# Two of five blocks of K transposed by permutes and DMA instead of TensorE, with a zero column and a warm-up on constants

## The chip, the core and the metric

The kernel runs on one core of a Trainium2 chip. The metric is device time in microseconds (us), the median of several runs. The engines are named as in the profile: PE (TensorE matmul) and PEld (its weight loads), DVE (VectorE), ACT (ScalarE), POOL (GpSimd) and SP (SyncE, which here only issues DMAs).

## What is computed

The input is one sequence of 2048 positions with 640 channels. A long convolution over the sequence is followed by a dense layer with Mish:

```
x  = A_q
h  = x + layernorm(x) * y                  # y, per channel:
     k_shift = sum over t of 4 taps: k shifted by t * shift_k[:, t]
     kv      = k_shift * v
     y       = causal_conv(kv, ssm_k) + kv * ssm_D     # length 2048, by FFT in the reference
h2 = h + mish(layernorm(h) @ w1 + b1) @ w2 # F = 1728
```

## The kernel before

Position s is 16 p + a, with p the partition (128) and a = 0 to 15. Channels are split into five blocks of 128 (`NDC`), and these into three chunks: blocks 0 and 1, blocks 2 and 3, block 4. The convolution is a two-stage transform written as matmuls:

- `k1pe`/`k1ev`: the filter `ssm_k` (loads d_n0 to d_n4) is transposed by PE into PSUM and copied out ("evicted") by DVE or ACT. `s1kpe`/`s1kev` is its first transform stage, `s2kpe`/`s2kev` its second, which multiplies by the table G (loads d_g0 to d_g7).
- `ktpe`/`ktev`: K, the raw k, lies with positions on partitions (loads d_k0 to d_k3). For the shift along the sequence PE transposes it, eight 128x128 tiles to a unit, x for the first half of a (h = 0) and y for the second (h = 1). Each block b gets a buffer `kt_s[b]` with three parts of 128 columns for each of eight tiles: the two halves, and the second half moved on by one column with a zero in front, which POOL copies (`ktsh`).
- `wsh`: the four taps as small banded matrices, a product of a mask and the coefficients (`coef`), ten of them on POOL. `kspe` multiplies `kt_s` by them in PE, and `kv` multiplies the result by v on DVE, from PSUM into the buffer that held the raw k. So kv also waits until the raw k has been read.
- `s1vpe`, `s2vpe`: the two stages for kv. `sw`: DMAs that exchange odd and even partitions of the transformed filter (`sw0` for chunk 0 in four pieces, `sw1` and `sw2` in two). `p1`, `p2`: the products of the two spectra, on POOL and DVE. `i1pe`, `i2p`: the inverse stages.
- Then, by groups of positions, the layernorms, `m1pe` (w1), `hb` (Mish on ACT), `m2pe` (w2), `res` and the store. Fourteen DMA transposes (`trd`) bring the normalised rows into the layout that m1pe needs; they are there before and after.

Every operation is an `OP` with a name, engines that may run it, and what it depends on. The text `ORDER` gives each name and an engine (t PE, v DVE, a ACT, p POOL, d the DMA queue on SP, s that on ACT). `_schedule` walks through it and gives each a start by the file's own figures, and the instructions are issued in the order of these starts. Each engine and each queue runs its own in that order. A pair of names ending in x and y is one `unit` in two PSUM banks; there are eight banks (`R_PS`), so PE can be at most eight evictions ahead.

`wm` is a burst of eleven matmuls on a zeroed tile (`wz`, a DVE memset) ahead of everything else on PE. `dcpe` then needs d_dr, and `k1pe0y` needs d_n0.

## Time and profile before

| | us |
|---|---|
| median of 3 runs | 221.82 |
| lowest and highest | 221.41, 222.13 |
| span of the profiled execution | 219.6 |
| PE busy in it | 212.6 |
| DVE busy | 145.1 |
| ACT busy | 133.1 |
| POOL busy | 75.6 |

The span is the time from the first to the last instruction of one execution; no other time is listed for that execution, and the median of the runs stands 2.2 us above its span. Matmuls are pipelined, so that PE counts as busy while one streams in and another drains, and it can also be called busy when it runs at less than its best rate. The table by stretch shows in which part of the kernel which engine has no idle time. The chain of work that ended last is followed back from the last instruction, at each step to what released it. The loads fill the DMA engines up to about 35 us.

### The profile page before, as it was taken

How to read it: one execution, taken by the hardware profiler on the slowest of the kernel's cores; microseconds unless marked ns; L12 is line 12 of the kernel's file. 1: busy time of each engine (PE TensorE's matmuls, PEld its weight loads, DVE VectorE, ACT ScalarE, POOL GpSimd, SP SyncE). 2: the span in 40 equal slices, each digit the busy share in tenths (PEclk: the TensorE clock that was granted, in tenths of full speed). 3: DMA queues.
4: the chain of work that ended last, by engine and by line, in shares of the span. 5: the costliest groups of instructions: out<-in, count | busy, mean ns of one | idle time of the engine just before them, and what ended most of it. 6: DMA issues, size and time to landing. Idle time of an engine off the chain costs nothing.

```text
span 219.6 us, 6285 instructions
## 1 busy us (share of the span) xinstructions
PE 212.6 (97%) x2611; PEld 157.8 (72%) x2618; DVE 145.1 (66%) x324; ACT 133.1 (61%) x265; POOL 75.6 (34%) x112
## 2 busy tenths in 40 slices
PE   8999999999989999999999999999999999999993
PEld 2899889999879999899876644566554444656672
DVE  0799999999999999989699889883210000213023
ACT  2488899999999999997881178600036475300000
POOL 0079997089844007124883371411000000000000
PEclk9999999999999999999999999999999999999999
DMA  6999993417999906996004401552720000000113
GB/s 213 375 419 414 412 403 130 98 23 174 192 263 285 380 10 217 325 359 105 0 0 64 91 14 45 50 103 60 86 79 19 0 3 0 0 0 3 54 60 125
DMA packets 32876, 31.03 MB, mean 141 GB/s; under 512 B 19024, under 2 KB 29264, under 8 KB 32464
## 3 DMA queue, kind: packets, MB, share of 16 engines
q1 hardware_dynamic: 32384, 30.43, 46.3%
q8 instruction: 20, 0.33, 0.7%
q10 hardware_dynamic: 368, 0.20, 0.4%
q14 instruction: 8, 0.07, 0.1%
q0 software_dynamic: 96, 0.00, 0.0%
HBM read 20.47 MB, written 2.62 MB: 105 GB/s over the span
## 4 chain that ended last, share of the span: by engine, by line
PE 76%; ACT 11%; DVE 5%; issue 3%; SPq 2%; DMA 1%; DVEq 0%; ACTq 0%
PE ps L943 26%; PE ps L910 26%; ACT uk L428 8%; PE ps L813 4%; ACT uv L428 3%; PE ps L756 3%; PE ps L757 3%; PE ps L635 2%; PE ps L561 2%; PE ps L473 2%; PE ps L590 2%; DMA xa<-uk 1%; DVE ra L613 1%; PE ps L931 1%; DVE uv L716 1%
## 5 line engine op out<-in xcount | busy, mean ns | idle before, releaser
L910 PE MATMUL ps<-G 128*128 128x512 bf16 (+1 forms) x319 | 58.5, 336 | 0.3
L943 PE MATMUL ps<-rn,uv 128*128 128x320 bf16 (+2 forms) x415 | 58.5, 299 | 0.1
L915 ACT ACTIVATE uv<-ps,b1s 128x512 bf16<-128x512 f32 (+1 forms) x65 | 35.6, 607 | 36.6 <-PE ps L910 34.8
L943 PEld LDWEIGHTS <-uv 128*128 128x128 bf16 x416 | 39.2, 98 | 18.5 <-issue 1.6
L910 PEld LDWEIGHTS <-G 128*128 128x128 bf16 x325 | 31.1, 98 | 24.0 <-issue 0.9
L428 ACT CAST uk<-ps 128x512 bf16<-128x512 f32 (+1 forms) x91 | 47.2, 703 | 1.9 <-PE ps L562 1.4
L948 DVE TENSOR_TENSOR xb<-ps,xb 128x320 bf16<-128x320 f32 (+2 forms) x12 | 5.6, 488 | 42.6 <-ACT uv L915 24.3
L428 ACT CAST uv<-ps 128x512 bf16<-128x512 f32 (+2 forms) x54 | 28.6, 766 | 0.0
L430 DVE CAST uk<-ps 128x512 bf16<-128x512 f32 (+2 forms) x32 | 20.1, 661 | 0.6 <-ACT uk L428 0.5
L756 PE MATMUL ps<-a,uv 128*128 128x128 bf16 x160 | 18.7, 219 | 0.4 <-DVE uv L716 0.3
L756 PEld LDWEIGHTS <-uv 128*128 128x128 bf16 x160 | 17.8, 114 | 0.9 <-DVE uv L716 0.5
L837 POOL TENSOR_TENSOR r<-ve,mhalf 128x1 f32<-128x1 f32 x16 | 9.7, 613 | 25.0 <-DVE ve L834 24.9
L430 DVE CAST uv<-ps 128x512 bf16<-128x512 f32 (+2 forms) x28 | 17.2, 669 | 0.2 <-ACT uv L428 0.2
L948 DVE TENSOR_TENSOR xa<-ps,xa 128x320 bf16<-128x320 f32 x12 | 5.6, 486 | 14.0 <-PE ps L943 13.9
L613 DVE TENSOR_TENSOR ra<-ps,rb 128x512 bf16<-128x512 f32 x20 | 12.9, 683 | 0.3 <-ACT uv L428 0.3
L720 POOL TENSOR_TENSOR rn<-rn,uv 128x1024 bf16<-128x1024 bf16 x5 | 10.6, 2127 | 7.2 <-PE ps L697 7.2
L697 PE MATMUL ps<-uv,G 128*128 128x64 bf16 (+1 forms) x256 | 12.2, 197 | 0.8 <-ACT uv L428 0.6
L662 PE MATMUL ps<-uk,G 128*128 128x160 bf16 x128 | 12.4, 230 | 0.3 <-ACT uk L428 0.2
L697 PEld LDWEIGHTS <-G 128*128 128x128 bf16 x256 | 10.8, 96 | 1.4 <-issue 1.0
L428 ACT CAST rb<-ps 128x512 bf16<-128x512 f32 (+1 forms) x30 | 11.3, 464 | 0.7 <-PE ps L813 0.4
L561 PE MATMUL ps<-cst,ra 128*64 128x128 bf16 x160 | 10.7, 219 | 0.4
L562 PE MATMUL ps<-cst,ra 128*64 128x128 bf16 x160 | 10.9, 222 | 0.0
(111 smaller groups left out, 375.7 us busy)
## 6 DMA issues: line engine op xcount, KB each, us to landing
G<-tab_g SPq DMA_DIRECT2D x8, 512.0 KB, 14.1
rn<-in_A_ssm_k_dram SPq DMA_DIRECT2D x5, 512.0 KB, 6.3
ra<-in_A_k_dram SPq DMA_DIRECT2D x4, 640.0 KB, 11.4
rb<-in_A_v_dram SPq DMA_DIRECT2D x2, 1280.0 KB, 13.9
G<-in_B_w_dram SPq DMA_DIRECT2D x5, 432.0 KB, 7.3
rn<-in_B_w_dram SPq DMA_DIRECT2D x1, 2080.0 KB, 13.4
rn<-uk SPq DMA_DIRECT2D x8, 256.0 KB, 4.3
rb<-uk SPq DMA_DIRECT2D x8, 256.0 KB, 4.5
```

Source lines behind the costliest of these rows:

```text
L428: nc.scalar.copy(o, i)
L430: nc.vector.tensor_copy(o, i)
L561: nc.tensor.matmul(ps[0:64, k, :], lhs, mc, start=True, stop=True)
L562: nc.tensor.matmul(ps[64:128, k, :], lhs, ms, start=True, stop=True)
L613: nc.vector.tensor_tensor(kv_w[:, m, k:32:2, 8 * h:8 * h + 8, :], ps.rearrange("p (l t d) -> p d t l", l=4, t=8), raw_v[:, 8 * h:8 * h + 8 ...
L662: nc.tensor.matmul(ps[:, o:o + 160], g_v[:, f, :], KA[:, :, f, :], start=True, stop=True)
L697: nc.tensor.matmul(ps[:, fl * n:fl * n + n], g_v[:, f0 + h * kf + fl, :], VX[x][:, :, f0 + h * kf + fl, :], start=True, stop=True)
L756: nc.tensor.matmul(pz[:, k, :], V[c.i][:, dg // 4, :, dg % 4], a12[:, 0, :], start=True, stop=False)
L910: nc.tensor.matmul(ph[:, 0:w], w1[:, dc, fc * P:fc * P + P], lnhT_of(u)[:, dc, 0:w], start=(dc == 0), stop=(dc == NDC - 1))
L915: nc.scalar.activation(hb_of(u)[:, fc, 0:w], rt.tile[:, 0:w], ACT.Mish, bias=b1s[:, fc:fc + 1], scale=1.0)
L943: nc.tensor.matmul(po[:, 0:d1 - d0], hb_of(u)[:, fc, tl * P:(tl + 1) * P], w2[:, fc, d0:d1], start=False, stop=(fc == NFC - 2))
L948: nc.vector.tensor_tensor(x, rt.tile[:, 0:d1 - d0], x, ALU.add)
```

## The change

Blocks 3 and 4 of K (`KX`) are no longer transposed by PE. For each of the two halves, `kp` copies the 1024 values of each partition into the order of the tiles (three times on POOL, once, kp4_0, on ACT), into buffers that are free at that time (xb and hc), and `kx` is one DMA transpose of 128 x 1024 from there straight into `kt_s`, on SP's queue. Four PE units (ktpe3, ktpe4) and their four evictions go.

For all five blocks the moved copy goes as well: `kt_s` now has 272 columns to a tile, a zero column (15) in front of the second half, so that a view that begins one column earlier (15 to 143) is the moved half. The five `ktsh` go. The second `wsh` of each block moves from xb into the place that this leaves.

The burst has ten matmuls on a constant of ones that is written before the program's own first instruction, and `wz` goes. d_n0 is loaded by two DMAs of 64 partitions each. `wsh4_0` moves from POOL to DVE. The whole text of `ORDER` is another one, and so the order on all engines changes in all stages.

```diff
-    wz = hc_t[:, 1280:1280 + P]
-    wz4 = wz.unsqueeze(1).to_broadcast([P, 4, P])
-    c_wz = OP("wz", ("dve", 0.95), emit=lambda e: nc.vector.memset(wz, 0.0), prio=-5)
+    ones = nc.const_aps.tensor(1.0, [P, 512], BF16)
...
-        for _ in range(11):
-            nc.tensor.matmul(ps[:, 0:512], wz, wz4, start=True, stop=True)
+        for _ in range(10):
+            nc.tensor.matmul(ps[:, 0:512], ones[:, 0:P], ones, start=True, stop=True)
...
-    kt_s = [t[:, 0:3072].rearrange("p (g a t) -> p g a t", g=8, a=3) for t in at_uv]
-    wsh = [[x.rearrange("p (l n) -> p l n", l=4) for x in (t[:, 3072:3776], xb[:, 704 * m:704 * m + 704])] for m, t in enumerate(at_uv)]
+    kt_s = [t[:, 0:2176].rearrange("p (g n) -> p g n", n=272) for t in at_uv]
+    wsh = [[t[:, 2176 + 704 * k:2880 + 704 * k].rearrange("p (l n) -> p l n", l=4) for k in range(2)] for t in at_uv]
+    KX = [3, 4]
...
-            nc.gpsimd.memset(kt_s[i][:, :, 2, 0:1], 0.0)
+            nc.gpsimd.memset(kt_s[i][:, :, 15:16], 0.0)
...
+            for h in range(2):
+                nc.sync.dma_start(raw_n[0][64 * h:64 * h + 64], n_view[0, 16 * h:16 * h + 16])
...
-        def shf(e, t=kt_s[b]):
-            nc.gpsimd.tensor_copy(t[:, :, 2, 1:128], t[:, :, 1, 0:127])
...
+            def kpf(e, b=b, h=h):
+                src = raw_k[:, h * 8 * D:(h + 1) * 8 * D].rearrange("p (n k r) -> p k r n", k=2, r=20)[:, :, 4 * b:4 * b + 4, :]
+                o = KP[b, h].rearrange("p (k r n) -> p k r n", k=2, r=4)
+                if e == "act":
+                    nc.scalar.copy(o, src)
+                else:
+                    (nc.vector if e == "dve" else nc.gpsimd).tensor_copy(o, src)
...
+                nc.sync.dma_start_transpose(kt_s[b][:, :, 144 - 128 * h:272 - 128 * h], KP[b, h])
...
-                    nc.tensor.matmul(o, t[:, q, h, :], w[:, 0:128], start=True, stop=False)
-                    nc.tensor.matmul(o[:, 0:48], t[:, q, 0 if h else 2, :], w[:, 128:176], start=False, stop=True)
+                    nc.tensor.matmul(o, t[:, q, 144 - 128 * h:272 - 128 * h], w[:, 0:128], start=True, stop=False)
+                    nc.tensor.matmul(o[:, 0:48], t[:, q, 144:272] if h else t[:, q, 15:143], w[:, 128:176], start=False, stop=True)
...
+s1vpe0_0y:t kx4_0:d d_g5:d d_g0:d d_g6:d kx4_1:d s2kev_10y:a s2kev_10x:a s2kev_19x:a s1vev1_2y:v s1vpe1_0y:t sw0_1:d s1vpe0_3x:t s1vpe0_0x:t
```

The queue on SP, from the loads of G and V on, was this (rb from A_v is v; a pair of rn from uk is a piece of sw0):

```order
L541 DMA G_95<-tab_g 128x2048 x3
L535 DMA rb_104<-in_A_v_dram 128x5120
L541 DMA G_95<-tab_g 128x2048 x4
L678 DMA rn_105<-uk_102 64x16x128
L679 DMA rn_105<-uk_102 64x16x128
L678 DMA rn_105<-uk_102 64x16x128
L679 DMA rn_105<-uk_102 64x16x128
```

Now it is this (the transposes are kx4_0, kx4_1, and then kx3_0 and kx3_1 together):

```order
L534 DMA rb_104<-in_A_v_dram 128x5120 x2
L546 DMA G_95<-tab_g 128x2048 x2
L616 DMA_TRANSPOSE uv1_101<-hc_99 128x8x128
L546 DMA G_95<-tab_g 128x2048 x3
L616 DMA_TRANSPOSE uv1_101<-xb_98 128x8x128
L693 DMA rn_105<-uk_102 64x16x128
L694 DMA rn_105<-uk_102 64x16x128
L616 DMA_TRANSPOSE uv1_101<-xb_98 128x8x128 x2
```

The last three loads of G (d_g5, d_g0, d_g6) have come to stand behind kx4_0, which waits for the permute on ACT, and the transposes of block 3 behind the first piece of sw0, which waits for evictions of s2k.

On POOL the same part of the program, the wsh (L516), the moved copies (L601) and a layernorm (L791 to L793), was this:

```order
L516 TENSOR_TENSOR xb_98<-cst_72,coef_79 128x704 x3
L516 TENSOR_TENSOR uv1_101<-cst_72,coef_79 128x704
L516 TENSOR_TENSOR uv0_100<-cst_72,coef_79 128x704
L601 COPY uv1_101<-uv1_101 128x8x127
L516 TENSOR_TENSOR xb_98<-cst_72,coef_79 128x704
L601 COPY uv0_100<-uv0_100 128x8x127
```

Now it is this, with the permutes kp4_1 and kp3_0, and later kp3_1 (L611):

```order
L515 TENSOR_TENSOR uv1_101<-cst_72,coef_79 128x704 x2
L515 TENSOR_TENSOR uv0_100<-cst_72,coef_79 128x704 x2
L611 COPY xb_98<-ra_103 128x1024 x2
L806 TENSOR_SCALAR ve1_82<-mv1_81 128x1
L807 TENSOR_TENSOR r1_86<-ve1_82,mhalf_84 128x1
L808 TENSOR_SCALAR nmr1_87<-mv1_81,r1_86 128x1
L515 TENSOR_TENSOR uv0_100<-cst_72,coef_79 128x704
L611 COPY xb_98<-ra_103 128x1024
```

Five wsh come first now, then two permutes; wsh0_0 (the single row of L515 for uv0) and kp3_1 follow, and the remaining wsh stand behind these.

More of the change, by code (lines that the diff above doesn't have):

```diff
@@ L26 @@
 ORDER = """
-d_id:s wz:v d_dr:s d_sk:s d_go:d wm:t d_n0:d d_n2:d d_n3:d d_x0:d d_n1:d d_n4:d d_k2:d dcpe:t warm:a dcev:v dq0:v k1pe0y:t k1pe0x:t k1pe2y:t d_k3:d
-k1ev0y:v d_k1:d dq2:v k1pe2x:t k1ev0x:v k1ev2y:v k1ev2x:a s1kpe0_0x:t s1kev0_0x:v d_k0:d s1kpe0_3x:t s1kpe0_1y:t s1kpe0_2x:t s1kpe0_2y:t s1kpe2_2x:t
-s1kpe2_3x:t s1kpe2_0y:t s1kev0_3x:a ln1_2:v s1kev0_2y:a s1kev0_2x:a dq1:v cfpe:t kz:p ln1p2:p s1kev2_3x:a dq3:v s1kev2_2x:a ln1_3:v s1kev0_1y:v dq4:v
-d_g4:d k1pe3y:t k1ev3y:a coef:a d_v1:d wsh4_0:p ln1p3:p k1pe1x:t d_g3:d d_g2:d k1ev1x:a wsh2_1:p wsh0_0:p wsh4_1:p wsh1_1:p wsh3_1:p wsh2_0:p d_g1:d
@@ L171 @@
 ]
[L172 removed]
+_COUNT = [('s1.pe|kspe|k1pe|i1pe', 32), ('ktpe', 32), ('s2kpe_21', 4), ('s2kpe', 12), ('s2vpe0', 32), ('s2vpe1', 20), ('i2pa', 4), ('i2pb', 4), ('i2pc', 4), ('wm', 20), ('trpe', 10), ('m1pe', 10), ('m2q', 8), ('m2pe', 26), ('cfpe', 18), ('dcpe', 8), ('b1pe', 2)]
 _COUNT = [('m1pex1', 20), ('m1pex', 40)] + [(f'(?:{k})[^xy]*$', n) for k, n in _COUNT] + [(f'(?:{k})[^xy]*[xy]$', n // 2) for k, n in _COUNT]
[L174 to L176 removed]
+_MARK, _BLOCK, _FETCH = 197, 253, [(8, 4.7), (32, 6.2), (45, 3.0), (76, 5.5), (1e9, 4.2)]
+_PORT_DVE = r"(p[12]_|wsh|kp|dadd|wb|h\d)"
+_PORT_POOL = r"(p[12]_|wsh|lnx|kp|dadd)"
 _HOP = 0.04
@@ L621 @@
     d_g = [DMA(f"d_g{i}", 0.525e6, emit_g(i), deps=d_n[:1], prio=0.6, lat=4.9) for i in range(8)]
[L623 removed]
+    d_small = OP("d_small", ("pool", 3.0), [kt_done[KX[0] if KX else 0, 1]], emit=emit_small2, lat=6.0)
     k1_pes, k1_by = [], []
```

180 lines of the change are left out of this document (93 added, 87 removed).

## The prediction

> **What bounds the kernel now.** I read the page first, then busy time by stretch, then the chain that ended last, then the timeline of the first 40 us. The page gives the span, and TensorE (PE) as the fullest engine:
>
> ```profile
> span 219.6 us, 6285 instructions
> PE 212.6 (97%) x2611; PEld 157.8 (72%) x2618; DVE 145.1 (66%) x324; ACT 133.1 (61%) x265; POOL 75.6 (34%) x112
> ```
>
> A busy PE isn't proof that PE sets the pace, so the table by stretch (span columns: PE, weight loads, DVE, ACT, POOL, granted clock, DMA share, GB/s) decides:
>
> ```profile
> 30.00:40.00 10.00, 9.89 (x233) 9.53 (x233) 10.00 (x18) 9.52 (x21) 6.82 (x13) 1.00 0.65 221
> 40.00:50.00 10.00, 9.96 (x228) 9.65 (x226) 9.73 (x18) 10.00 (x23) 5.04 (x3) 1.00 0.23 46
> 50.00:60.00 10.00, 9.58 (x243) 8.48 (x241) 9.84 (x18) 10.00 (x22) 9.71 (x5) 1.00 0.87 186
> 60.00:70.00 10.00, 9.03 (x183) 8.34 (x180) 10.00 (x18) 10.00 (x23) 4.54 (x4) 1.00 0.98 265
> 70.00:80.00 10.00, 9.70 (x173) 9.48 (x171) 10.00 (x16) 10.00 (x22) 0.00 (x0) 1.00 0.68 252
> 80.00:90.00 10.00, 10.00 (x153) 9.24 (x150) 9.44 (x17) 9.89 (x23) 4.38 (x5) 1.00 0.56 196
> 140.00:180.00 40.00, 39.84 (x245) 22.45 (x245) 11.64 (x33) 11.49 (x20) 3.50 (x6) 1.00 0.34 54
> ```
>
> From 30 to 80 us ACT and DVE have no idle time to speak of: they copy PSUM out, and PE (9.0 to 9.9 of 10) waits for free banks. From 80 us on PE is full while ACT and DVE have room. So there are two laws: before 80 us a microsecond of ACT and DVE work counts, after 80 us one of PE work. The change sits wholly in the first part.
>
> **The change part by part.** First the start, from the timeline and the DMA issues (the last two rows: the weights of d_dr and the load d_n0, with microseconds from issue to landing at the end):
>
> ```profile
> 0.30 0.10 POOL L980 MEMSET const-bfloat16-1.0<- 128x1 bf16 x1
> 0.72 0.35 ACTq L479 DMA_DIRECT2D cst<-tab_cst  x1
> 0.72 1.98 SPq L538 DMA_DIRECT2D rn<-in_A_ssm_k_dram  x3
> 0.81 0.11 DVE L467 MEMSET hc<- 128x64 uint32 x1 [0.81 <-PEq L980]
> 0.98 4.88 PE L473 MATMUL ps<-hc 128*128 128x512 bf16 x11 [0.98 <-DVE warm L463]
> 1.10 0.48 ACTq L480 DMA_DIRECT2D d_row<-in_A_ssm_D_dram  x1
> 5.79 0.26 PE L486 MATMUL ps<-d_row,cst 32*128 32x5 bf16 x4
> 5.98 2.30 PE L635 MATMUL ps<-cst,rn 128*128 128x128 bf16 x32
> d_row<-in_A_ssm_D_dram ACTq DMA_DIRECT2D x1, 1.2 KB, 4.0
> rn<-in_A_ssm_k_dram SPq DMA_DIRECT2D x1, 512.0 KB, 4.4
> ```
>
> The warm-up waits for a DVE memset until 0.98. Constants that POOL has written by 0.40 let it begin with the queues, at 0.72 (0.26 sooner), and one matmul fewer takes off 4.88/11 = 0.44. The burst would end near 5.1 instead of 5.8. The data allow about that: d_row lands at 1.10 + 4.0 = 5.1, d_n0 at 0.72 + 4.4 = 5.1. But d_n0 is now two DMAs, and each issue costs SP 1.98/3 = 0.66, so its second half, and all loads behind, may come up to 0.66 later. Gain 0.04 to 0.7; I take 0.45, nearer the d_row bound, since d_n0's bytes are the same. From the chain, these pieces are used here and below (K's transposes, an s2kpe unit, an s2vpe0 unit, a DMA wait, full-speed matmuls of 512 columns):
>
> ```profile
> 18.42 4.60 PE ps L590 x72
> 41.42 0.21 PE ps L662 x3
> 41.63 0.31 PE ps L697 x8
> 63.85 3.15 DMA xa<-uk
> 170.20 10.74 PE ps L910 x49
> ```
>
> 10.74/49 = 0.22 us at full speed against 0.44 in the burst: all eleven warm-up matmuls ran at half rate while the granted clock read 1.00, and the 32 that follow at 5.98 took 2.30/32 = 0.07, full rate. So full rate came between 4.4 and 5.0 us after the burst's first matmul, and a burst of 10 x 0.44 = 4.4 may fall just short: the first 16 transposes would then pay twice, 16 x 0.07 = 1.1 us more, and the start would lose 0.65 instead of gaining 0.45. That is the start's lower bound. The Trainium skill (TensorE: Matmul & The Clock Gate, What's actually happening) has full rate begin after some 3.4 us of activity, in a window that runs freely and so shifts between runs. By that rule the shorter burst suffices and the 0.45 stands; by this trace's 4.4 to 5.0 it is a near thing.
>
> Next the transposes of blocks 3 and 4: ktpe3 and ktpe4, four units of eight, go. 32 x 4.60/72 = 2.04 us of PE. That is before 80 us, so it is worth what ACT and DVE give up. Their rows (timeline; for the rest groups by line and form):
>
> ```profile
> 13.71 1.92 DVE L430 COPY rn<-ps 128x1024 bf16<-128x1024 bf16 x3
> 19.60 1.93 ACT L428 COPY uv<-ps 128x1024 bf16<-128x1024 bf16 x2 [0.74 <-PE ps L590]
> 25.93 3.56 ACT L428 CAST uk<-ps 128x512 bf16<-128x512 f32 x7
> L601 POOL COPY uv<-uv 128x1016 bf16<-128x1016 bf16 x5 | 5.1, 1029 | 0.0
> L516 POOL TENSOR_TENSOR uv<-cst,coef 128x704 bf16<-128x704 bf16 x5 | 6.8, 1366 | 0.8 <-ACT coef L428 0.8
> L716 DVE TENSOR_TENSOR uv<-uv,uk 128x1024 bf16<-128x1024 bf16 x12 | 8.1, 700 | 0.0
> ```
>
> An eviction costs DVE 1.92/3 = 0.64, ACT 1.93/2 = 0.97 for 1024 columns and 3.56/7 = 0.51 for 512. By the suffixes of the two lists, ACT loses three ktev (-2.9) and gains one k1ev (+0.97), two s2kev and one s1vev (+1.5) and the permute kp4_0; DVE loses one ktev, one k1ev, two s2kev and one s1vev (5 x 0.64 = -3.2) and gains wsh4_0. kp4_0 reads SBUF with a stride that no row shows: between one ACT copy of that size (0.97) and twice that; I take 0.97. wsh4_0: between a DVE product of two SBUF operands, 0.70 x 704/1024 = 0.48, and POOL's 1.37; I take 0.8, nearer DVE's. ACT +0.5, DVE -2.4, together -1.9. The two share one pool of evictions, so half each: the stage ends 0.95 sooner; I take 0.9. Bounds: ACT alone sets the pace, 0.5 later; PE does after all, 2.04 sooner.
>
> POOL loses five ktsh (5.1) and one wsh (1.37) and gains three kp, each between a ktsh (1.03) and a two-operand op of its size (1.366 x 1024/704 = 1.99): 0.5 to 3.4 less. POOL idles 66% and is nowhere late, so nothing, as long as wsh0_0, which now stands behind two kp, is in time.
>
> The DMAs. SP is one queue; kx4_0 stands ahead of d_g5, d_g0 and d_g6, and kx3_0 behind sw0_1. The rows: DMA transposes of hc (issue time, then landing), the stretch in which one of them ran alone, the last table load with its landing, sw0_1's issue, and two places of PE:
>
> ```profile
> L849 SPq DMA_TRANSPOSE G<-hc x14: 1200/1211/2649, 98.3 to 156.5; - x14
> DMA to landing us min/median/max: 2.6/2.7/4.1
> 146.00:147.00 1.00, 1.00 (x10) 0.73 (x9) 1.00 (x3) 0.00 (x0) 0.00 (x0) 1.00 0.80 153
> 24.44 0.32 SPq L541 DMA_DIRECT2D G<-tab_g  x1
> G<-tab_g SPq DMA_DIRECT2D x1, 512.0 KB, 12.3
> 37.09 0.65 SPq L678 DMA_DIRECT2D rn<-uk  x1
> 40.33 0.44 PE L662 MATMUL ps<-uk,G 128*128 128x160 bf16 x4
> 40.91 0.10 PEld L609 LDWEIGHTS <-uv 128*128 128x128 bf16 x1
> ```
>
> A five-block transpose holds the 16 DMA engines for 0.8 us; eight blocks 1.3. The loads ended at 24.44 + 12.3 = 36.7; kx4_0 puts 1.3 into that stream, and g0, now second last of it (one load, about 1.3, less), still lands near 36.7. PE first asks for g0 at s2kpe_1y, 40.33 before; ahead of it now stand four ktpe (2.04), two s2kpe (2 x 0.21) and one kspe (about 0.33) fewer, and the start is 0.45 sooner: 37.1. A margin of 0.4 where it was generous. I book 0; if each of the two transposes in that stream took twice its time, 1 to 2. kx4_0 waits for kp4_0, which is ACT's 27th eviction or so, about 27 us; the loads ahead of it last beyond that, so the DMA engines don't run dry: 0.
>
> The second half keeps its work: product pieces (nine on POOL as before), the inverse stages and the MLP have the same instructions, and d_x1's wait stands in front of one weight load instead of two. 0.
>
> Sum: 0.45 + 0.9 = 1.35 sooner. The profiled span of 219.6 becomes 218.25; the median of the runs, 221.82, lies 2.2 above the span, so 220.5.
>
> **The rivals.** *PE gains in full* (faster): if the new order feeds ACT and DVE so that PE sets the pace, the whole 2.04 shows: 221.82 - 0.45 - 2.04 = 219.3. For it: PE's 9.9 of 10 at 30 to 50 us. Against: 9.0 at 60 to 70. There the chain waits 3.15 for a transfer of sw1; sw1_0 no longer has sw2_0 ahead of it on SP, which may make that shorter by up to a third, 218.3 at the extreme.
>
> *Nothing shows*: ACT, 10.00 of 10, sets the pace alone with its +0.5 against the start's 0.45, or the loads' margin of 0.4 is used up: 221.8.
>
> *The transposes come late* (slower): PE is in order, and kspe3_1x needs kx3_0 and kx3_1. Its place was 40.91; ahead of it now are four ktpe fewer, ten s2kpe (2.1), two kspe (0.65) and seven s2vpe0 (2.2) more: 40.91 - 2.04 + 4.95 - 0.45 = 43.4. sw0_1 went out at 37.09 and may again; two issues (1.3), kx3_0's issue (1.2 to 1.9 for eight blocks) and kx3_1 is issued at 39.6 to 40.3. Landing takes 2.7 to 4.1 x 8/5 = 6.6: 42.3 to 46.9. It decides from 43.4 on. All evictions behind that PE unit wait: at most 3.5, in the middle some 2.5 with the gain still taken: 221.82 - 1.35 + 2.5 = 223.0. Against it: sw0_1's last eviction now comes sooner. The Trainium skill speaks for it (VectorE: DVE Perf Modes, The three transpose paths): it sends a 128x128 transpose to TensorE where PSUM will do, at 390 ns, and gives the DMA path 1309 ns. By that figure eight blocks would be an estimated 10.5 us and PE would wait some 7. The trace has five blocks landing in 2.7, so the row decides and the figure is not used.
>
> **How the numbers follow.** Forecast 0.40, PE in full 0.17, nothing 0.17, late transposes 0.26. About 0.3% (0.7 us) is what a measurement here can tell. Faster 0.40 + 0.17 = 0.57, same 0.17, slower 0.26. The likeliest case alone runs from 219.8 (start 0.7, evictions 1.3) to 221.1 (0.04 and 0.7). The range goes down through the case of PE in full to 218.5, near its extreme, and up into the late case, with half of its last microsecond, to 223.8.
>
> **What would show it.** Right: the first L486 near 5.3; 48 instead of 80 transposes of K; ACT and DVE full to about 79 and then a PE-full tail of unchanged length; the last i1 eviction about 1.3 sooner. Wrong: PE waiting for a DMA at a kspe3 or kspe4 unit or at an s2kpe of g0 between 35 and 45 us; first K transposes spaced at twice 0.07; kp rows far above 2 us on POOL or ACT; or, if the tail after 90 us differs by over 0.5, the law taken for it.

## The result, and the profile after

The changed kernel takes 224.41 us (median of 4 runs, 223.98 to 224.94) against 221.72 us before (4 runs, 221.41 to 222.13) on the same chip: a ratio of 1.0109 with a 95% interval of [1.0083, 1.0135]. That is 2.7 us slower by the medians, and 2.4 by the ratio. The forecast was 220.5, the range 218.5 to 223.8.

From the page of the changed kernel, the span and the busy times:

```profile
span 222.3 us, 6241 instructions
PE 212.8 (96%) x2585; PEld 156.8 (71%) x2585; DVE 145.1 (65%) x320; ACT 133.8 (60%) x265; POOL 76.8 (35%) x109
```

TensorE has 33 fewer weight loads (its matmul records, of which a few are missing before, fall by 26) and is not less busy; ACT is busier, DVE the same. The table by stretch (span columns as in the prediction: PE, weight loads, DVE, ACT, POOL, clock, DMA share, GB/s; the share counts a packet's time in the slice in which it starts, so it can pass 1):

```profile
30.00:40.00 10.00, 9.68 (x212) 9.22 (x212) 9.08 (x15) 10.00 (x22) 8.84 (x11) 1.00 1.14 263
40.00:50.00 10.00, 9.73 (x241) 9.36 (x236) 9.82 (x17) 10.00 (x23) 4.33 (x3) 1.00 0.82 111
60.00:70.00 10.00, 8.46 (x181) 7.46 (x175) 9.42 (x17) 10.00 (x23) 8.08 (x11) 1.00 1.04 257
140.00:180.00 40.00, 40.00 (x247) 22.30 (x246) 15.43 (x43) 12.78 (x21) 3.41 (x6) 1.00 0.23 42
```

ACT is full in all rows up to 70 (before, it had 9.52 from 30 to 40), but DVE now stands 0.9 us between 30 and 40 and 0.6 between 60 and 70, where it was full. The DMA engines carry more from 30 to 50.

Three stretches hold the whole difference: up to TensorE's first matmul of s1k (L566; L561 before), from there to the end of the last eviction of i1 (the stretch that the prediction said ACT and DVE pace), and the rest. The start of the changed kernel, in its timeline:

```profile
0.76 4.43 PE L472 MATMUL ps<-const-bfloat16-1.0 128*128 128x512 bf16 x10 [0.76 <-PEq L995]
5.12 0.27 PE L485 MATMUL ps<-d_row,cst 32*128 32x5 bf16 x4
6.29 3.57 PE L650 MATMUL ps<-cst,rn 128*128 128x128 bf16 x32 [0.90 <-DMA rn<-in_A_ssm_k_dram]
9.80 0.24 PE L566 MATMUL ps<-cst,xa 128*64 128x128 bf16 x1
```

The burst and dcpe are close to where they were forecast. Then TensorE waits 0.90 for d_n0, and its 32 transposes take 3.57 us where they took 2.30. The first s1k matmul is at 9.80, not 8.21. The end of the middle stretch is the last copy of PSUM into uk: before it is on DVE at 86.74 + 1.29 = 88.03, after it is on DVE at 89.52 + 0.69, which is 90.22 before rounding:

```profile
86.74 1.29 DVE L430 CAST uk<-ps 128x512 bf16<-128x512 f32 x2 [0.48 <-ACT uk L428]
```

```profile
89.52 0.69 DVE L431 CAST uk<-ps 128x512 bf16<-128x512 f32 x1 [0.74 <-PE ps L772]
```

The table by stretch for the middle and the rest, of before and then of after:

```profile
8.21:88.03 79.82, 77.46 (x1653) 72.82 (x1651) 77.89 (x136) 77.09 (x154) 48.01 (x47) 1.00 0.75 250
88.03:219.64 131.61, 127.91 (x915) 81.13 (x920) 65.30 (x182) 54.52 (x110) 27.11 (x55) 1.00 0.29 68
```

```profile
9.80:90.22 80.42, 76.28 (x1620) 70.89 (x1620) 77.16 (x131) 77.91 (x155) 48.78 (x43) 1.00 0.92 272
90.22:222.33 132.11, 128.38 (x922) 81.00 (x920) 65.99 (x183) 53.39 (x108) 27.46 (x56) 1.00 0.23 57
```

So the start is 1.59 us later, the middle 0.60 longer, the rest 0.50 longer: 2.7. In the middle DVE and ACT together are busy for 154.98 before and 155.07 after: the 1.9 us that the change was to take from them are not taken. Where they went, from the groups by line and form:

```profile
L609 ACT COPY hc<-ra 128x1024 bf16<-128x1024 bf16 x1 | 2.4, 2350 | 0.0
L611 POOL COPY xb<-ra 128x1024 bf16<-128x1024 bf16 x3 | 6.9, 2303 | 0.0
L515 DVE TENSOR_TENSOR uv<-cst,coef 128x704 bf16<-128x704 bf16 x1 | 1.2, 1207 | 0.0
```

The permute on ACT took 2.35 us (booked 0.97), those on POOL 2.30 (bounded by 1.99), wsh4_0 on DVE 1.21 (booked 0.8).

### The profile page after: what moved, and what is told of

Same layout as the page of the kernel before. It is cut to its first block, busy times and chain, and to the rows that moved or that the text cites. A ratio compares the mean times of both kernels' runs of the same rounds, so it can differ in the third digit from the quotient of the medians.

```text
span 222.3 us, 6241 instructions
## 1 busy us (share of the span) xinstructions
PE 212.8 (96%) x2585; PEld 156.8 (71%) x2585; DVE 145.1 (65%) x320; ACT 133.8 (60%) x265; POOL 76.8 (35%) x109
## 4 chain that ended last, share of the span: by engine, by line
PE 78%; DVE 8%; ACT 7%; DMA 2%; issue 2%; SPq 0%; DVEq 0%; ACTq 0%
PE ps L958 26%; PE ps L925 26%; ACT uv L429 5%; PE ps L772 4%; PE ps L771 4%; PE ps L828 4%; PE ps L566 3%; PE ps L677 3%; ACT uk L429 2%; DVE uv L431 2%; DVE uk L431 2%; DMA rn<-in_A_ssm_k_dram 2%; PE ps L650 2%; PE ps L594 2%; DVE st L801 1%
## 5 line engine op out<-in xcount | busy, mean ns | idle before, releaser
L930 ACT ACTIVATE uv<-ps,b1s 128x512 bf16<-128x512 f32 (+1 forms) x65 | 35.5, 613 | 37.1 <-PE ps L925 36.7
L429 ACT CAST uk<-ps 128x512 bf16<-128x512 f32 (+1 forms) x93 | 48.9, 710 | 3.3 <-PE ps L567 2.3
L429 ACT CAST uv<-ps 128x512 bf16<-128x512 f32 (+2 forms) x55 | 30.1, 862 | 0.0
L431 DVE CAST uk<-ps 128x512 bf16<-128x512 f32 (+1 forms) x30 | 19.0, 670 | 1.7 <-PE ps L772 0.7
L515 POOL TENSOR_TENSOR uv<-cst,coef 128x704 bf16<-128x704 bf16 x9 | 12.8, 1437 | 15.0 <-ACT coef L429 15.0
L431 DVE CAST uv<-ps 128x512 bf16<-128x512 f32 (+2 forms) x27 | 16.6, 673 | 0.0
L677 PE MATMUL ps<-uk,G 128*128 128x160 bf16 x128 | 13.0, 230 | 0.3 <-ACT uk L429 0.3
L838 DVE TENSOR_TENSOR rb<-rb,ra 128x640 bf16<-128x640 bf16 x16 | 7.4, 480 | 5.8 <-ACT ra L815 5.8
L828 PE MATMUL ps<-uk,ra 128*128 128x256 bf16 (+1 forms) x96 | 10.9, 255 | 0.0
```

Source lines behind the costliest of these rows:

```text
L429: nc.scalar.copy(o, i)
L431: nc.vector.tensor_copy(o, i)
L515: (nc.gpsimd if e == "pool" else nc.vector).tensor_tensor(out, a, b, ALU.mult)
L677: nc.tensor.matmul(ps[:, o:o + 160], g_v[:, f, :], KA[:, :, f, :], start=True, stop=True)
L828: nc.tensor.matmul(py, t2m[:, t2, ri, :], Z[c.i][:, :, ri * NT + t2, :], start=(ri == 0), stop=(ri == 1))
L930: nc.scalar.activation(hb_of(u)[:, fc, 0:w], rt.tile[:, 0:w], ACT.Mish, bias=b1s[:, fc:fc + 1], scale=1.0)
```

## The experiments

All ratios are against the kernel before, measured beside it on the same chip, with 95% intervals. "First s1k" and "last i1" are the two borders above, read from each run's profiled execution, one for each run. In the fourteen kernels with one load of d_n0 and ten warm-up matmuls the first s1k lies anywhere between 7.57 and 8.35, so a difference of a few tenths there says nothing.

| run | ratio | interval | span | first s1k | last i1 |
|---|---|---|---|---|---|
| changed kernel | 1.0109 | 1.0083 to 1.0135 | 222.3 | 9.80 | 90.22 |
| a1_one_load | 1.0062 | 1.0046 to 1.0078 | 221.3 | 7.57 | 88.92 |
| a2_bridge | 1.0081 | 1.0054 to 1.0109 | 222.2 | 8.94 | 90.34 |
| a3_dense | 1.0158 | 1.0105 to 1.0212 | 223.5 | 10.55 | 91.44 |
| b1_warm | 0.9988 | 0.9970 to 1.0007 | 220.5 | 7.67 | 88.89 |
| b2_split | 1.0051 | 1.0027 to 1.0075 | 222.2 | 9.99 | 90.59 |
| c1_halo | 0.9993 | 0.9973 to 1.0012 | 219.7 | 8.25 | 88.15 |
| d1_plain_copy | 1.0052 | 1.0028 to 1.0075 | 220.4 | 7.99 | 88.56 |
| d4_pe_transposes | 1.0107 | 1.0071 to 1.0142 | 222.0 | 7.85 | 88.99 |
| a13_dense_one | 1.0134 | 1.0079 to 1.0190 | 221.7 | 7.90 | 89.62 |
| e1_dense_act | 0.9999 | 0.9973 to 1.0025 | 219.6 | 8.35 | 87.64 |
| e2_dense_act_dma | 1.0079 | 1.0050 to 1.0108 | 221.7 | 8.25 | 89.71 |
| f1_loads_first | 1.0089 | 1.0063 to 1.0116 | 222.0 | 7.95 | 89.94 |
| f2_pool_permutes | 1.0195 | 1.0171 to 1.0219 | 224.4 | 7.83 | 92.47 |
| k1_kp_dve | 1.0080 | 1.0057 to 1.0103 | 223.2 | 7.71 | 91.00 |
| g1_one_block | 1.0032 | 1.0008 to 1.0055 | 221.0 | 8.32 | 89.54 |
| g2_between_code | 1.0056 | 1.0035 to 1.0077 | 220.8 | 7.73 | 89.30 |
| g3_spread | 1.0119 | 1.0093 to 1.0145 | 221.5 | 7.58 | 90.02 |

### The start: a1, a2, b1, b2

**a1_one_load** is the changed kernel with

```
-            for h in range(2):
-                nc.sync.dma_start(raw_n[0][64*h:64*h+64], n_view[0, 16*h:16*h+16])
+            nc.sync.dma_start(raw_n[b], n_view[b])
```

> The changed kernel with d_n0 as one DMA again. Theory S (the start): the halved load lands about 1 us late, TensorE stands 0.9 us, and behind that hole the 32 first transposes run at half rate (3.57 us instead of 2.30). Then one DMA brings the first s1k matmul from 9.80 to about 7.7 and the time from 224.4 to 222.3 to 222.8. If the shorter burst, not the hole, keeps the rate low, the transposes begin near 5.4 but still take 3.4: s1k near 8.9, 223.5. Rival E (ACT and DVE hold the pace and a late start is swallowed by their later work): 224.0 or more, whatever the start does.

Its timeline begins

```profile
5.12 0.25 PE L485 MATMUL ps<-d_row,cst 32*128 32x5 bf16 x4
5.31 2.33 PE L646 MATMUL ps<-cst,rn 128*128 128x128 bf16 x32
7.57 0.24 PE L562 MATMUL ps<-cst,xa 128*64 128x128 bf16 x1
```

No hole, full rate, first s1k 2.23 us sooner than in the changed kernel: theory S is right on what one load does to the start, and ten matmuls sufficed here. But only 1.0 us of it (1.0109 to 1.0062) reaches the end. A new wait stood in the way; it comes below.

**a2_bridge** keeps the two loads and warms up with 13 matmuls:

```
-        for _ in range(10):
+        for _ in range(13):
```

> The changed kernel with d_n0 still in two DMAs, and 13 warm-up matmuls instead of 10, so that the burst (13 x 0.443 = 5.8 us from 0.76) reaches past the landing at 6.2. Theory S, the hole costs the rate: transposes begin near 6.7, 0.4 later than now, but take 2.3: first s1k near 9.0 instead of 9.8, 223.6. If the transposes are slow for another reason than the hole: first s1k near 10.2 and 224.8.

Its transposes are back at full rate and in two pieces, each behind its load:

```profile
6.04 1.24 PE L650 MATMUL ps<-cst,rn 128*128 128x128 bf16 x16
7.80 1.21 PE L650 MATMUL ps<-cst,rn 128*128 128x128 bf16 x16 [0.51 <-DMA rn<-in_A_ssm_k_dram]
```

16 in 1.24 is 0.08 apiece against 3.57/32 = 0.11 behind the hole. First s1k at 8.94, as expected (9.0); 1.0081, near the 223.6 expected. That the hole alone costs the rate is not shown, though. The first row below is of a3 (further down), which has the changed kernel's start: it has a hole of 0.80 and runs at full rate behind it. The second is of d4, which has one load and no hole and is 0.3 slower than the kernel before:

```profile
6.19 1.18 PE L650 MATMUL ps<-cst,rn 128*128 128x128 bf16 x16 [0.80 <-DMA rn<-in_A_ssm_k_dram]
5.32 2.60 PE L650 MATMUL ps<-cst,rn 128*128 128x128 bf16 x32
```

In the trace of d4 the transposes start 0.107 us apart up to 6.37 and 0.062 apart from there. So the moment at which full rate comes differs between executions of the same burst from 0.77: it is 3.7 in a13, inside the burst, and 6.4 in d4. In a3 it came between 5.1 and 6.3, and in the changed kernel's profile not before 9.6: there the transposes start 0.107 apart throughout. A hole that puts off a full rate which had not yet come would fit these rows; each is one execution, and why it does so in one and not in the other stays open.

**b1_warm** is the kernel before with the ten matmuls on constants and nothing else:

```
-    wz = hc_t[:, 1280:1280 + P]
+    ones = nc.const_aps.tensor(1.0, [P, 512], BF16)
-        for _ in range(11):
+        for _ in range(10):
```

> The kernel before with the new warm-up alone: ten matmuls on constants from 0.76, d_n0 one DMA. By the prediction's start term: first transposes 0.45 sooner at full rate, 221.3. If ten are too few: the transposes begin near 5.4 at half rate, first s1k near 8.9 instead of 8.2, 222.3. If a start that is sooner is swallowed by ACT and DVE: 221.7.

First s1k comes at 7.67, 0.54 sooner in this one execution, and the time stays: 0.9988, interval across 1. ACT shows why:

```profile
15.54 1.56 ACT L359 CAST uk<-ps 128x512 bf16<-128x512 f32 x3 [1.97 <-PE ps L491]
```

It now stands 1.97 us before 15.54 (0.74 at that place before): the next blocks of the filter are still on their way. DVE's first statistics of x wait for their load to the same moment in both kernels, first before, then b1:

```profile
10.02 0.89 DVE L786 BATCH_NORM_STATS2 st<-x 128x6 f32<-128x320 bf16 x2 [0.66 <-DMA x<-in_A_q_dram]
10.10 0.89 DVE L715 BATCH_NORM_STATS2 st<-x 128x6 f32<-128x320 bf16 x2 [1.27 <-DMA x<-in_A_q_dram]
```

The loads, not the warm-up, time the work up to there.

**b2_split** adds the halved d_n0 to b1:

```
-        return lambda: nc.sync.dma_start(raw_n[b], n_view[b])
+            for h in range(1 if b else 2):
+                q = 128 if b else 64
+                nc.sync.dma_start(raw_n[b][q * h:q * h + q], n_view[b, 16 * h:16 * h + q // 4])
```

> The kernel before with the whole of the change's start: ten warm-up matmuls on constants and d_n0 in two DMAs. Theory S: the second half lands about 1 us later, TensorE stands, and the first transposes run at half rate: first s1k near 9.8 instead of 8.2, as in the changed kernel. What this costs at the end tells how much of the change's 2.7 is the start: between 0.8 (half swallowed, as the warm-up alone won nothing with a start 0.5 sooner) and 1.6 (all): 222.4 to 223.3. If the start doesn't matter, 221.7.

First s1k at 9.99 and 1.0051. Against b1 (0.9988) that is 0.0063, 1.4 us, for a start 2.3 us later. In its profile the first 16 transposes came behind d_n0 and the next 16 waited 1.34 us more for the next block. So the start part alone is worth 1.0 to 1.4 us of the 2.7, in either order; each of the two differences carries about 0.7 us of noise.

### The permute: a3, a13, d1, e1, k1

**a3_dense** reads all four permutes without the stride (a plain copy of 1024 elements, so K's blocks 3 and 4 hold other numbers):

```
-                src = raw_k[...].rearrange("p (n k r) -> p k r n", ...)[:, :, 4*b:4*b+4, :]
+                src = raw_k[:, h*8*D + 1024*(b-3):h*8*D + 1024*(b-2)]
-                o = KP[b, h].rearrange(...)
+                o = KP[b, h]
```

> The changed kernel with the four permutes kp read without the stride (a plain copy of 1024 elements a partition, so blocks 3 and 4 of K are other numbers). Price of the stride: kp on ACT 0.97 instead of 2.35, on POOL 1.03 instead of 2.30. Theory P (the permute on ACT is what ate the eviction term): 1.38 us of ACT less, shared with DVE 0.7, so 223.7. Rival Q (the queues: kx4_0 stands in front of three loads of G on SP and waits for kp4_0 until 28.5): the loads come 1.4 us sooner too, and more than 1.2 is won, 223.2 or less. Rival N (ACT and DVE have slack there): under 0.3.

It does not answer. The copies cost 1.08 on ACT and 1.04 on POOL, but its start went wrong further than the changed kernel's: the second sixteen transposes waited 1.55 us, and TensorE's clock was granted at 0.86 in the next stretch:

```profile
8.92 1.70 PE L650 MATMUL ps<-cst,rn 128*128 128x128 bf16 x16 [1.55 <-DMA rn<-in_A_ssm_k_dram]
10.00:20.00 10.00, 9.99 (x198) 9.18 (x197) 8.64 (x20) 7.46 (x13) 2.21 (x2) 0.86 1.02 411
```

**a13_dense_one** is the same with one load of d_n0:

```
-            for h in range(2):
-                nc.sync.dma_start(raw_n[0][64 * h:64 * h + 64], n_view[0, 16 * h:16 * h + 16])
+            nc.sync.dma_start(raw_n[b], n_view[b])
```

> One load of d_n0 and the four permutes kp as plain copies without the stride (so other numbers in blocks 3 and 4 of K). ACT pays 1.08 instead of 2.35 for kp4_0, POOL about 1.05 instead of 2.30 each. Theory P (the stride ate the eviction term): 1.27 of ACT, shared 0.6: 222.9. Theory C on top: TensorE comes 0.6 sooner to the point near 40 where its code is late, and the transposes start 1.3 sooner; if the code's landing follows the transposes the 0.6 shows, if it is fixed by the loads ahead nothing does: 223.5.

1.0134, with times from 223.5 to 226.1, is too scattered for a price; its profile (221.7, the lowest of them) has TensorE standing 1.5 us near 40. Neither expectation is met, and both runs are left out of what follows.

**d1_plain_copy** is a1 with plain copies in place of the DMA transposes (so blocks 3 and 4 stay untransposed, and the zero that POOL writes for them moves to their last 128 columns, not shown):

```
-                nc.sync.dma_start_transpose(kt_s[b][:, :, 144-128*h:272-128*h], KP[b, h])
+                nc.sync.dma_start(kt_s[b].rearrange("p g n -> p (g n)")[:, 1024-1024*h:2048-1024*h], KP[b, h])
```

> As the run with one load of d_n0 (223.5 beside 222.3 of the kernel before, 1.0062), but the four DMA transposes kx are plain DMA copies of the same 256 KB each, so blocks 3 and 4 of K stay untransposed. In the run with one load TensorE stood 1.2 to 1.4 us inside kspe2_0x near 40 us, at instruction 1462 = 197 + 5 x 253 of its stream, with no releaser named, while an 'instruction' transfer went through the DMA engines. Theory C (the transposes hold the DMA engines, about 2 us each, and TensorE's next block of code lands late): the stand goes, 1.2 to 1.4 less, 222.2. Rival B (the bytes do it, or it is no code at all): the stand stays and the time with it, 223.3 to 223.6.

The stand near 40 us is gone, as theory C has it, and the profiled span is 0.9 shorter than a1's. The time is not what it expected: 1.0052 is where rival B stood (1.005 to 1.006), and the ratios of the two runs (1.0062 and 1.0052) don't separate. The pair e1 and e2 does.

**e1_dense_act** is d1 with the stride taken from kp4_0 on ACT alone (so this quarter of blocks 3 and 4 holds other numbers besides):

```
-                src = raw_k[...].rearrange(...)[...]
-                o = KP[b, h].rearrange(...)
+                src = raw_k[:, h * 8 * D + 1024 * (b - 3):h * 8 * D + 1024 * (b - 2)] if e == "act" else raw_k[...].rearrange(...)[...]
+                o = KP[b, h] if e == "act" else KP[b, h].rearrange(...)
```

> As the run with plain copies in place of the DMA transposes (1.0052 of before, no stand for code), with one more edit: kp4_0 on ACT reads without the stride (1.08 us instead of 2.35; other numbers in that block). It prices the eviction term alone: theory P, 1.27 us of ACT shared by ACT and DVE, 0.64 sooner, about 1.0023; and the gaps of DVE near 28 and 29 us (0.41 and 0.67), when eight banks wait behind kp4_0, shrink. If ACT is not what counts: 1.005.

0.9999: 0.0053 less, 1.2 us. The interval reaches 1.0025, so the times alone don't exclude the 0.64 expected; the profiles show more than half of ACT's saving of 1.27. The middle stretch of d1 and then of e1:

```profile
7.99:88.56 80.57, 76.48 (x1621) 70.98 (x1620) 77.31 (x132) 77.90 (x155) 48.80 (x43) 1.00 0.84 278
```

```profile
8.35:87.64 79.29, 76.15 (x1621) 70.86 (x1620) 76.90 (x132) 76.65 (x155) 48.85 (x43) 1.00 0.85 282
```

ACT is busy 1.25 less and the stretch is 1.28 shorter; it ends 0.92 sooner, as e1's began 0.36 later. The rows of DVE say why it isn't halved. In the changed kernel, right behind kp4_0 (26.13 to 28.48), DVE stands twice:

```profile
30.20 0.69 DVE L431 COPY uv<-ps 128x1024 bf16<-128x1024 bf16 x1 [0.40 <-PE ps L594]
31.58 0.66 DVE L431 CAST uk<-ps 128x480 bf16<-128x480 f32 x1 [0.68 <-PE ps L677]
```

While ACT is in the permute, the banks that its own list names stay full, TensorE stops, and DVE runs out of work: 1.08 us. What TensorE waited for in the changed kernel from 26 to 32 us:

```profile
PE ps L594 <- ACT uk L429: 0.7, 1, 0.7
PE ps L677 <- ACT uk L429: 0.3, 1, 0.3
```

d1 has the same two waits. In e1 TensorE has none from 24 to 32, and DVE has no such gap.

**k1_kp_dve** is a1 with one word of the order changed:

```
- kp4_0:a
+ kp4_0:v
```

> One load of d_n0 and kp4_0 on DVE instead of ACT, stride and all. No row shows the strided copy on DVE. If it costs there what it costs on ACT (2.35), the time stays at 1.006. If DVE takes about 1.1 (a plain pass of 1024 elements at the 0.64 to 0.68 of its evictions, and a little more), the stage is 1.2 sooner until TensorE stands for its code near 40 us, which gives most of it back: 1.003 to 1.006.

The strided copy takes DVE 1.22 us (its one row of that line), half of what it takes ACT. The time is 1.0080: TensorE then stood 2.0 us near 42, and what was won is gone, a little more than expected.

### The DMA transposes: e2, f1, f2

**e2_dense_act_dma** is e1 with the DMA transposes back:

```
-                nc.sync.dma_start(kt_s[b].rearrange("p g n -> p (g n)")[:, 1024-1024*h:2048-1024*h], KP[b, h])
+                nc.sync.dma_start_transpose(kt_s[b][:, :, 144-128*h:272-128*h], KP[b, h])
```

> One load of d_n0, the DMA transposes as in the change, and kp4_0 on ACT without its stride (1.08 us instead of 2.35; other numbers in that block). The same without the DMA transposes was 0.9999. Theory C (the DMA transposes make TensorE wait for its code): TensorE comes to the point near 40 us 1.3 sooner and stands there 1.3 to 1.7: 1.005 to 1.007, hardly less than with the stride (1.0062). If the transposes cost nothing: 1.000 to 1.001.

1.0079 against 0.9999: the four DMA transposes cost 1.8 us. The waits of TensorE, from its timeline and its weight loads:

```profile
41.92 0.18 PE L625 MATMUL ps<-uv 128*128 128x48 bf16 x1 [2.10 <-issue]
41.93 1.10 PEld L677 LDWEIGHTS <-G 128*128 128x128 bf16 x16 [2.22 <-issue]
```

"issue" names no engine and no data, and in the stretch from 40 to 42 all engines drain:

```profile
40.00:42.00 2.00, 0.07 (x2) 0.07 (x2) 0.47 (x1) 1.05 (x3) 0.00 (x0) 1.00 1.17 202
```

Counted through the records of TensorE's matmuls and weight loads, the stand is three or four behind instruction 1462 of its stream in every run that has it, also in a2, which has three more of each at its start. The trace's DMA records hold one transfer of 16 KB of kind "instruction" every 253 instructions, of about 1.0 us. In the queue rows from 39 to 41 us of e2 (packets, MB, their time as a share of 16 engines) it runs beside DMA transposes and the swap sw0_1:

```profile
q1 hardware_dynamic: 1981, 0.50, 126.5%
q8 instruction: 1, 0.02, 3.2%
```

With the start of instruction 1209 (253 ahead), the transfer that follows it, and the moment at which TensorE goes on past 1462:

```
run                instr. 1209   code transfer      goes on   after landing
before                34.40      35.15 to 36.17     no stand
e1 (plain copies)     35.27      35.48 to 36.41     no stand
changed kernel        37.92      39.88 to 40.88      42.49       1.61
a1                    35.76      38.64 to 39.66      41.25       1.59
a2                    37.06      39.92 to 40.93      42.42       1.49
e2                    35.73      39.44 to 40.47      41.92       1.45
f1                    36.45      39.50 to 40.45      42.16       1.71
k1                    37.08      40.74 to 41.76      43.35       1.59
g1                    35.03      37.92 to 39.56      41.13       1.57
```

Seven stands of 0.5 to 2.3 us, and each ends 1.45 to 1.71 us behind the landing of that transfer. (a3, a13, g2 and g3 have it too: 1.1, 1.5, 0.3 and 0.3 us, ending 1.69, 1.51, 1.44 and 1.36 behind it. In e2 the 35.73 itself stands behind an earlier one of 0.6 us, 1.50 behind its landing.) TensorE waits for its own code, whose transfer starts 2 to 4 us behind its request instead of 0.2 to 0.8. e1 and e2 differ in the DMA transposes alone, so here it is these that delay it.

Loads do the same. In the kernel before, the four code transfers that begin between 12 and 32 us, while the loads fill the DMA engines, start 3.1 to 3.6 us behind their requests, and TensorE stands for one of them, at instruction 955. Its transfer ran from 25.30 to 26.38, and TensorE went on 1.51 behind the landing:

```profile
27.89 0.11 PEld L562 LDWEIGHTS <-rn 128*64 128x64 bf16 x1 [0.41 <-issue]
```

So the wait is not new with the change; the DMA transposes carry it past the end of the loads. The kernel's own planner has it as well: `_schedule` holds TensorE for a fetch every `_BLOCK` = 253 instructions.

**f1_loads_first** is a1 with d_g5, d_g0 and d_g6 ahead of kx4_0 in the order of SP:

```
- kx4_0:d d_g5:d d_g0:d d_g6:d kx4_1:d
+ d_g5:d d_g0:d d_g6:d kx4_0:d kx4_1:d
```

> One load of d_n0, and on SP the loads of g5, g0 and g6 ahead of kx4_0 instead of behind it. In the run with one load kx4_0 kept loads of G from the DMA engines for about 2.7 us (30.8 to 33.4), the last ended at 37.9, and TensorE's code asked for at 35.8 landed at 39.7, 1.2 to 1.4 late. Theory C: the loads now end near 35, but kx4_0 and kx4_1 then run from 35 to 40, just when the code is asked for; so the stand stays at 0.7 to 1.5 and the time at 1.005 to 1.006. If loads, not transposes, delay the code: the stand goes, 1.001.

TensorE stands 1.4 to 1.6 us at the same instruction, so the last three loads are not what delays the code there. 1.0089 is worse than the 1.005 to 1.006 expected.

**f2_pool_permutes** is f1 with kp4_0 on POOL and kx4_1 ahead of kx4_0:

```
- kp4_0:a ... kx4_0:d kx4_1:d
+ kp4_0:p ... kx4_1:d kx4_0:d
```

> One load of d_n0, the loads of G ahead of the DMA transposes, and kp4_0 on POOL instead of ACT (kx4_1 ahead of kx4_0, as POOL does kp4_0 last). ACT gives up 2.35 us: by the law that ACT and DVE together set the pace 1.2 sooner than the run with the loads first, that is 1.000 to 1.001 of before. If POOL becomes late (wsh2_0 and wsh3_1 now stand behind 2.3 us more; kspe2_0x asks near 39.6) it waits there instead and nothing is won: 1.005.

1.0195, far above both guesses. Not wsh2_0 but raw K itself is what it waits for: kp4_0, last of POOL's permutes, ends at 34.4, and until then the kv products may not overwrite what it reads.

```profile
32.12 2.30 POOL L611 COPY hc<-ra 128x1024 bf16<-128x1024 bf16 x1
35.20 0.57 PE L677 MATMUL ps<-uk,G 128*128 128x160 bf16 x6 [3.94 <-DVE ra L628]
```

### The order, and single blocks: c1, d4, g1, g2, g3

**c1_halo** is the kernel before, in its order, with the zero column (no ktsh) and the warm-up on constants. It is the changed code, with one load of d_n0, and

```
-KX = [3, 4]
+KX = []
 ORDER: that of before, less
- wz:v and every ktsh
```

> The kernel before in its own order, with two parts of the change: the warm-up on constants and the zero column (no ktsh copies, 5.1 us less of POOL). Blocks 3 and 4 stay on TensorE. The prediction booked nothing for POOL: then this stands with the warm-up alone (0.9988 of before), 222.0. If the copies held up kspe units through wsh0_0 and wsh0_1 on POOL: up to 0.7 sooner, 221.3.

0.9993: five copies less on POOL are worth nothing, as booked.

**d4_pe_transposes** is the changed order with KX = [], so that blocks 3 and 4 go through TensorE again (one load of d_n0):

```
-KX = [3, 4]
+KX = []
- every kp and kx
+ ktev0y:a ktpe3y:t ktev3y:a ktpe4y:t ktev4y:v ktpe3x:t ktev3x:a ktpe4x:t ktev4x:v
```

> The changed kernel and its order, one load of d_n0, but blocks 3 and 4 of K by TensorE again: four ktpe units with their evictions (two on ACT, two on DVE) in place of the permutes and DMA transposes. Against the run with one load (1.0062): ACT -2.35 + 1.94, DVE +1.28, TensorE +2.04. By the law of evictions +0.4 later, 1.008; by theory C the stand of 1.2 to 1.4 near 40 us goes, so together about 0.9 sooner, 222.6 (1.0015). If TensorE's 2.04 count in full, 223.9 and above.

1.0107. There is no stand for code, but the new order itself is no better than the old one: the middle stretch is 81.1 us (79.9 in c1), and one wait of 1.1 us for ACT (uv, L930) in the MLP belongs to this run alone. It shows that the transposes' cost is not the only one. It also leaves a rival that no run here settles: that the new order itself costs time. Without DMA transposes, without a strided copy and with one load, d4 is as slow as the changed kernel. But its four ktpe units stand in an order that wasn't made for them, so what the order costs can't be read from it. A sign of it in e1 is that DVE is busy 9.34 of 10 us from 60 to 70, where it was full before.

**g1_one_block** is c1 with block 3 alone by the new way, its permutes on POOL and its DMA transposes behind all loads:

```
-KX = []
+KX = [3]
- ktpe3y:t ktev3y:a ktpe3x:t ktev3x:v
+ kp3_0:p wsh0_1:p ... kp3_1:p ln1p1:p ... kx3_0:d kx3_1:d kspe3_1x:t
```

> The kernel before in its own order with the zero column and the warm-up on constants (0.9993), and block 3 alone by the new way: two permutes on POOL in the place of the five ktsh copies, two DMA transposes behind all loads on SP, the kspe3 units after them. Sixteen transposes less on TensorE (1.02 us), ACT -0.97 and DVE -0.64 of evictions, nothing added to either. By the law of evictions with half each 0.8 sooner: 0.9955. If the transposes, 2.7 us each from about 36, make kspe3 (near 42) or TensorE's code wait: 1.000 and above.

1.0032. Slower where 0.9955 was hoped for, as its second guess had it. Sixteen transposes and two evictions less, and TensorE stands 1.8 us for code, by the table above:

```profile
41.13 0.23 PE L677 MATMUL ps<-uk,G 128*128 128x160 bf16 x1 [1.79 <-issue]
```

**g2_between_code** moves kx3_0 and kx3_1 apart and the four kspe3 units to about 47 us:

```
+    named['kx3_0'].deps.append(named['s2kev_5y'])
+    named['kx3_1'].deps.append(named['s1vev0_0x'])
- kx3_0:d kx3_1:d kspe3_1x:t
+ kx3_0:d sw0_1:d kx3_1:d ... kspe3_1x:t kv3_1x:v kspe3_0x:t kv3_0x:v kspe3_0y:t kv3_0y:v kspe3_1y:t kv3_1y:v s2kpe_14y:t
```

> As the run with one block by the new way (1.0032, TensorE standing 1.8 us for its code near 39 us), but kx3_0 waits for the eviction s2kev_5y (near 37) and kx3_1 for s1vev0_0x (near 41), behind TensorE's requests for code near 35.5 and 39.5, and the four kspe3 units stand near 47. Theory C: the stand is gone, 1.8 us less, and the time is 0.995 of before, faster than both kernels. If the code still lands late: 1.000 to 1.003. If the later kspe3 units leave ACT and DVE without work near 45, that shows as gaps there and the time is about 1.000.

SP did not hold kx3_0 back (issued at 27.1; the wait was only in the order's planning), kx3_1 went out at 38.2. The stand at 1462 fell to 0.3, but ACT stood 2.1 us from 47.5 to 51 instead, as the third guess had it, and the time is 1.0056, worse than its 1.000.

**g3_spread** spreads those four units and exchanges four evictions each way between ACT and DVE:

```
- s2kev_0y:a s2vev0_3y:a s2kev_20x:a s2kev_17y:a s2kev_14y:v s2kev_19x:v s2vev0_7x:v s2kev_15x:v
+ s2kev_0y:v s2vev0_3y:v s2kev_20x:v s2kev_17y:v s2kev_14y:a s2kev_19x:a s2vev0_7x:a s2kev_15x:a
```

> As the run with the DMA transposes between the requests for code (1.0056; code 0.3 us late near 39, ACT without work for 2.1 us from 47.5 to 51 while DVE evicted four kspe3 units in a row), but the kspe3 units apart from each other between 47 and 52, four evictions of that stretch moved from DVE to ACT and four near 43 from ACT to DVE. If the code's wait and that gap were what kept the gain: 2 us less than that run, 0.996. If ACT and DVE wait elsewhere instead, 1.000 to 1.004.

1.0119: a miss. ACT stood 1.5 us at 45.9 and DVE 0.9 at 55. Whether a better order could keep the gain of one block stays open. No version tried here beats the kernel before; b1 and c1 equal it, and e1, with other numbers in blocks 3 and 4.

## Why the prediction was wrong, point by point

**The two laws** held as to which engine is full: from 30 to 80 us ACT is, in the changed kernel too (9.89 to 10.00 in each 10 us); from 80 us on TensorE is, with 40.00 of 40 in the last row of the first table. In e1, where kp4_0 costs 1.08 and wsh4_0 1.20, half of (ACT +0.6, DVE -2.0) would be 0.7 sooner; the middle stretch is 0.53 shorter than before (79.29 against 79.82). What one long operation of ACT costs is another matter (the eviction term below).

**The start term, +0.45, is the first step that failed**: it was -1.59. Its warm-up half was right (0.76, 4.43 and 5.12 against 0.72, 4.4 and 5.3 forecast). The other half, d_n0 "assumed" at about 5.1 with up to 0.66 later, was read off one load: its halves landed so that TensorE began at 6.29, 1.0 later than with one load (5.31 in a1). The Trainium skill (DMA: Bandwidth & Descriptors, Rules for kernel authors) says of two transfers to the two halves of the partitions that they serialize, and that one transfer of all 128 is the better. The runs here agree as to which is better: with two, the first transposes come 0.3 us later in b2 (5.63 against 5.33 in b1) and 1.0 later here. The near thing about the clock was seen, but only half of it: with the shorter burst full rate did come late in some runs (6.4 in d4, 0.3 us lost), and in the one profile of the changed kernel 32 transposes behind the 0.9 us hole were slow instead of 16 (3.57 against 2.33). The Trainium skill's windows of some 3.4 us (TensorE: Matmul & The Clock Gate, What's actually happening) fit that: from 6.29 to the end of the last slow transpose is 3.57. And what a start is worth was taken as itself: 0.54 sooner in its profile bought nothing (b1), 2.2 to 2.3 later cost 1.0 to 1.4 (a1, b2), because the next loads time the work up to about 16 us.

**The eviction term, 0.9 sooner, is the second**: the middle stretch is 0.60 longer. Two prices were wrong. kp4_0 was given its lower bound, 0.97, "between one ACT copy and twice that", and was above the upper one: 2.35. wsh4_0 was 1.21, near POOL's 1.37 and not near DVE's 0.48. Together +1.8 us of ACT and DVE, which is nearly the whole of the 1.9 that was to be saved. (By the lists, the fourth eviction of 512 columns that changes engine is the net of two s2vev1 to ACT and one s1vev back; the sum is the same.) And "half each" was too little for one long operation: of the 1.27 us that the stride of kp4_0 cost ACT, 0.9 to 1.3 showed at the end of the stretch (e1).

**TensorE's 2.04** was rightly booked at nothing by itself: there are 48 transposes of K instead of 80, and TensorE's busy time is 212.8 against 212.6.

**POOL, nothing**: right for the changed kernel, though the permutes took 2.30, above both bounds, and POOL's first wsh came at 16.01 instead of 13.28. The condition named (wsh0_0 in time) was not the one that bites: raw K may not be overwritten before the last permute has read it, which f2 shows at 3.9 us.

**The DMAs, 0**: wrong in mechanism, small in the changed kernel. A transpose of eight blocks was given 1.3 us of the stream of loads; kx4_0 cost it more:

```profile
31.00:32.00 1.00, 1.00 (x18) 1.00 (x16) 0.42 (x1) 1.00 (x3) 1.00 (x1) 1.00 2.07 169
32.00:33.00 1.00, 1.00 (x20) 0.91 (x18) 1.00 (x3) 1.00 (x4) 1.00 (x2) 1.00 0.30 42
33.00:34.00 1.00, 1.00 (x23) 1.00 (x22) 1.00 (x2) 1.00 (x4) 1.00 (x1) 1.00 1.16 322
```

From 31 to 33 the DMA engines move 169 and 42 GB/s instead of some 400; in d1, with plain copies of the same bytes, no such slice from 26 to 35 is below 389. g0 was still in time, as s2kpe_1y came at 41.5 and not at 37.1. The transfer that came late was one that the prediction did not have: TensorE's code. It costs the changed kernel 0.5 us at 42, and 1.2 to 2.3 as soon as anything ahead of it gets faster, so that it is hidden behind the other two costs: taking the halved load away shows it (a1), and with the stride away as well it takes back all that was won (e2 1.0079, e1 0.9999).

**The tail, 0**: 0.50 longer (131.61 to 132.11), with TensorE busy 0.47 more. It is longer by 0.2 to 0.8 in a1, d1 and e1, which have the new order, and not in b1 and c1, which have the old one; which instructions of the order do it was not tried. This is just at the 0.5 that the prediction set as the mark against its law for the tail.

**The rivals.** Late transposes gave 223.0, the nearest time, but that is luck: kspe3_1x stands at 47.6 in the trace, not at 43.4, and waits for nothing there, though the transposes took 4.3 to 9.0 us to land where 6.6 was the bound. The other two were not seen.

Taken away one after the other, the costs give the ratios 1.0109, 1.0062 (one load, a1), 1.0052 (no DMA transposes, d1) and 0.9999 (no stride on ACT, e1): 1.0, 0.2 and 1.2 us of 2.4, each give or take some 0.7. With all three away the kernel is where it was. The share of the DMA transposes depends on what else is there: 0.2 us with the stride (a1 to d1), 1.8 without it (e2 to e1). Of the 1.35 of gain, 0.45 is swallowed by the loads; of the 0.9, the middle stretch of e1 does show 0.5, against which its start is 0.14 and its tail 0.33 longer. What the new order adds of its own stays open.

## What to carry to other kernels

Before an operation moves to another engine, look for a row with its access pattern, not only its size: the strided copy cost ACT 2.35 and POOL 2.30 where the dense one costs 1.08 and 1.04, and on an engine that also empties PSUM most of one long operation was paid for here. Count the instruction stream among the transfers that a busy DMA stretch delays: a stand with no releaser at a fixed instruction number is its sign, and a table of request, landing and resumption shows it. After removing one cost, look at the timeline again before adding up: here each of three costs covered part of the next.
